# A gated mix of a recurrent memory attention and a softmax attention: output projection in column tiles, last-token batches moved, exp steps from the prologue on

## The chip, the cores and the metric

The kernel runs on one core of one Trainium2 chip. The metric is the device time of one execution in microseconds (us). Three runs of the kernel before gave 2069.38, 2077.07 and 2085.11 us, so the median is 2077.07 us. The five engines of the core are called here as the profile calls them: PE (TensorE matmuls; PEld is its weight loads), DVE (VectorE), ACT (ScalarE), POOL (GpSimd) and SP (SyncE, which here only issues transfers).

## The reference, cut to what matters

There are two attentions over the same input x of 2048 tokens by 576 features, and a gate that mixes them.

```
# A: 64 segments of 32 tokens, one after the other; mem is 8 rows of 576
for s in range(64):
    h = concat([mem, x[s*32:(s+1)*32]])            # 40 x 576
    q, k, v = h @ Wq, h @ Wk, h @ Wv               # 32 heads of 128
    p = softmax(mask(q @ k.T * 128**-0.5))         # 40 x 40 per head
    o = (p @ v) @ Wo                               # 40 x 576
    mem = o[:8]                                    # needed by the next segment
    out_a[s*32:(s+1)*32] = o[8:]
# B: 32 heads of 18 over all 2048 tokens
q, k, v = split(x @ wqkv)
out_b = concat_heads(softmax(q @ k.T * 18**-0.5) @ v) @ wo
g = sigmoid((x * gate_w).sum(-1))
out = g * out_a + (1 - g) * out_b
```

A is a recurrence: a segment can't start before the eight memory rows of the one before are there. B has no such chain.

## The kernel before, in words

**Prologue.** It loads x, transposes it on PE (`ptx`), and projects it to the q, k and v of B (lines 218 and 244). Results go to DRAM (`qtd`, `ktd`, `vgd`). The last 8 tokens of each segment don't need the memory, so their q, k and v of A are computed here for all 64 segments, in four batches of 16 segments (lines 268 and 284), and stored as `vld`, `qld`, `kld`. The weights of A (14 MB in all) are loaded on the SP queue.

**Recurrence.** Each of the 64 segments handles 32 columns (8 memory rows and the first 24 tokens) and loads the other 8 tokens. It projects six times with `project` (line 462: 20 matmuls of 512 columns in four column tiles of 32, result `pvv`, copied to `tm` on DVE), turns q and k with PE transposes (`pt`), sends v through a transfer to `v_sb` (line 492), and forms the scores (`psh`) and their exponentials on ACT. The softmax follows in two halves b: sums (`pss`), reciprocals `rq` on DVE, their spread (`prb`), a product on DVE (line 546), and the values (`pso`), copied to `ot` on DVE (line 560). The output projection then runs 160 matmuls (line 569, `pbw`): for each of 32 heads five loads of 128x128 weights `wo`, each followed by a matmul of 40 columns. Three small DVE copies (lines 582 to 584) put the memory rows into the next segment's input `ht`; line 588 keeps the other rows in `otsg`, and every fourth segment `otsg` is turned (`pto`) and stored.

**Work of B between.** `b_steps` is a generator with 1024 steps. A step has two matmuls (`sb`, line 347) and one exponential of 128x1024 on ACT (line 356, about one us); every second step has four matmuls with the values (`ob`, line 328). `tick()` is called 16 times in a segment and takes 1024/65/16 = 0.98 steps on average. Eight times in the program the next group of heads is loaded, three transfers of 512 KB each on the POOL queue. All steps are over by the end of the recurrence.

**Epilogue.** For each of 16 tiles of tokens it reloads B's output (`otn`), multiplies with `wo` of B (line 620, `po`), mixes and stores.

**Order.** Each engine runs its own list of instructions strictly in order. A scheduler sets these lists when the program is built: it takes the program's operations by their dependences and its own estimates, so that neighbours in the code may change places. PSUM has three buffers for all tiles with the tag `pb`, two for `sb`, one for `ob`.

## Time and profile before

| | us |
|---|---|
| median of three runs | 2077.07 |
| the profiled execution's own time | 2076.26 |
| its span | 2074.6 |
| start to the first segment | 283 |
| 64 segments | 1738 |
| after the last output projection | 54 |

The three stages are read from the chain of waits: the first `pvv` starts at 282.7 us and the last `pbw` ends at 2021.0 us. The page's row PEclk gives the clock that PE was granted, as a share of full speed. A view by windows gives the same share, and each engine's busy time, for any stretch of the span. The busy time of PE counts a matmul until its end, so that a full PE is not PE at its best rate; the chain of waits, which gives how long a run of matmuls held the next one up, is used for durations.

### The profile page before, as it was taken

The numbers are of one execution on the slowest core, as the hardware profiler recorded it, in microseconds if no ns is written. First come the engines' busy times: TensorE is split into PE (matmuls) and PEld (weight loads), VectorE is DVE, ScalarE is ACT, GpSimd is POOL, SyncE is SP. The second block draws the span as 40 slices with busy tenths as digits, with TensorE's granted clock in tenths as the row PEclk, the third lists the DMA queues.
The fourth block names the chain that finished last, engine by engine and source line by source line (L and its number), as shares of the span: only waits on it lengthen the run. The fifth ranks groups of instructions, "written<-read, shape, count | busy, mean of one in ns | idle before, by whom it ended". The sixth has DMA issues, their size and how long they took to land.

```text
span 2074.6 us, 67963 instructions
## 1 busy us (share of the span) xinstructions
PE 1929.8 (93%) x30629; PEld 1081.4 (52%) x30646; DVE 831.7 (40%) x1867; ACT 1119.7 (54%) x1282; POOL 107.0 (5%) x268
## 2 busy tenths in 40 slices
PE   4699979999999899999999999999999999999996
PEld 2257845555555555555555555555555555555553
DVE  5123324443444344433444344444444444333445
ACT  1122256665556556555666566656665666565660
POOL 3000010000000000000000000000000000000000
PEclk9899988888888888888888899888889988888999
DMA  8643350001000110110000100010001000100016
GB/s 256 242 133 117 123 185 26 25 26 51 24 25 26 53 29 22 29 47 20 26 25 26 56 26 26 26 56 26 24 26 55 27 23 25 52 23 23 22 42 165
DMA packets 122582, 117.31 MB, mean 57 GB/s; under 512 B 60204, under 2 KB 112116, under 8 KB 119220
## 3 DMA queue, kind: packets, MB, share of 16 engines
q1 hardware_dynamic: 97940, 90.51, 13.9%
q10 hardware_dynamic: 20896, 9.87, 2.0%
q0 software_dynamic: 3456, 12.58, 1.8%
q8 instruction: 240, 3.93, 0.8%
q14 instruction: 50, 0.41, 0.1%
HBM read 58.91 MB, written 37.22 MB: 46 GB/s over the span
## 4 chain that ended last, share of the span: by engine, by line
PE 81%; DMA 9%; ACT 4%; DVE 3%; SPq 1%; issue 1%; POOL 0%; ACTq 0%; DVEq 0%
PE pvv L462 21%; PE pbw L569 16%; PE sb L347 15%; PE ob L328 9%; ACT etb L356 4%; PE pq L284 3%; PE psh L508 3%; PE pq L218 3%; PE pt L478 3%; DMA v_sb<-tm 3%; PE pso L552 2%; PE pq L268 2%; SPq L492 1%; PE prb L538 1%; DMA otn<-otd 1%
## 5 line engine op out<-in xcount | busy, mean ns | idle before, releaser
L356 ACT ACTIVATE etb<-sb 128x1024 bf16<-128x1024 f32 x1024 | 1029.9, 1026 | 690.4 <-PE sb L347 689.2
L347 PE MATMUL sb<-qtg,ktg 32*128 32x512 bf16 x2048 | 436.8, 423 | 16.4 <-DMA ktg<-ktd 11.2
L471 DVE CAST tm<-pvv 128x512 bf16<-128x512 f32 x384 | 265.3, 691 | 286.1 <-PE pvv L462 275.4
L569 PEld LDWEIGHTS <-wo 128*128 128x128 bf16 x10240 | 328.3, 106 | 77.0 <-issue 75.0
L569 PE MATMUL pbw<-ot,wo 128*128 128x40 bf16 x10240 | 355.7, 194 | 0.0
L462 PEld LDWEIGHTS <-ht 128*32 128x32 bf16 x7680 | 187.5, 96 | 191.3 <-issue 49.6
L328 PE MATMUL ob<-etb,vgi 128*32 128x512 bf16 x2048 | 243.9, 433 | 25.7 <-ACT etb L356 21.8
L347 PEld LDWEIGHTS <-ktg 32*128 32x128 bf16 x2048 | 99.9, 92 | 222.9 <-issue 192.1
L582 DVE CAST ht<-pbw 128x32 bf16<-128x32 f32 x63 | 12.0, 191 | 388.8 <-PE pbw L569 388.8
L560 DVE CAST ot<-pso 128x320 bf16<-128x320 f32 x256 | 115.3, 485 | 97.9 <-PE pso L552 97.6
L462 PE MATMUL pvv<-wv_m,ht 128*32 128x512 bf16 x2048 | 147.4, 382 | 0.0
L462 PE MATMUL pvv<-wq_m,ht 128*32 128x512 bf16 x2048 | 138.6, 385 | 1.4 <-DVE ht L582 0.3
L328 PEld LDWEIGHTS <-vgi 128*32 128x32 bf16 x2048 | 69.8, 94 | 127.1 <-issue 111.2
L462 PE MATMUL pvv<-wk_m,ht 128*32 128x512 bf16 x2048 | 134.6, 380 | 0.0
L454 POOL COPY qt<-xl 128x256 bf16<-128x256 bf16 x64 | 26.2, 410 | 1484.1 <-PE psh L508 1403.8
L218 PE MATMUL pq<-xT,wpk 128*128 128x512 bf16 x313 | 74.9, 399 | 19.2 <-ACT stg L228 16.8
L546 DVE TENSOR_TENSOR et<-et,prb 128x320 bf16<-128x320 bf16 x128 | 62.5, 488 | 75.1 <-PE prb L538 75.1
L552 PEld LDWEIGHTS <-v_sb 64*128 64x128 bf16 x2048 | 59.7, 99 | 56.9 <-issue 45.3
L552 PE MATMUL pso<-et,v_sb 64*128 64x40 bf16 x2048 | 73.6, 187 | 15.6 <-DVE et L546 8.0
L518 DVE TENSOR_TENSOR et<-et,cap 128x320 bf16<-128x320 bf16 x128 | 42.0, 329 | 114.7 <-ACT et L516 114.6
L508 PEld LDWEIGHTS <-kt 128*64 128x64 bf16 x2048 | 64.3, 111 | 35.8 <-issue 34.7
L508 PE MATMUL psh<-qt,kt 128*64 128x40 bf16 x2048 | 80.0, 189 | 0.2 <-DVE kt L483 0.2
(103 smaller groups left out, 1472.6 us busy)
## 6 DMA issues: line engine op xcount, KB each, us to landing
v_sb<-tm SPq DMA_DIRECT2D x512, 32.0 KB
wo<-in_A_Wo_dram SPq DMA_DIRECT2D x4, 1152.0 KB
wv_m<-in_A_Wv_dram SPq DMA_DIRECT2D x4, 1024.0 KB
wq_m<-in_A_Wq_dram SPq DMA_DIRECT2D x4, 1024.0 KB
wk_m<-in_A_Wk_dram SPq DMA_DIRECT2D x4, 1024.0 KB
qtd<-stg SPq DMA_DIRECT2D x8, 512.0 KB
ktd<-stg SPq DMA_DIRECT2D x8, 512.0 KB
vgd<-vt ACTq DMA_DIRECT2D x16, 256.0 KB
```

What stands on the lines that cost most here:

```text
L218: nc.tensor.matmul(pq[:, :], lhsT=wpk[:, c, :, :].rearrange("p j e -> p (j e)"), rhs=xT[:, c, t * QC:(t + 1) * QC], start=(c == 0), stop=( ...
L284: nc.tensor.matmul(pv[:, o:o + P], lhsT=lw, rhs=xL[:, cc, q * P:(q + 1) * P], start=(c == 0), stop=(c == NF),)
L328: mm = nc.tensor.matmul(ob[32 * j:32 * j + 32, :], lhsT=vg[:, kb * P + 32 * j:kb * P + 32 * j + 32], rhs=ets[j // 2][:, j % 2, :], start=( ...
L347: nc.tensor.matmul(sb[:, i, :], lhsT=ktg[32 * j:32 * j + 32, kb * P:(kb + 1) * P], rhs=qtg[32 * j:32 * j + 32, qc * QC:(qc + 1) * QC], sta ...
L356: nc.scalar.activation(out=etb[:, :, :], in_=sb[:, :, :], func=ACT.Exp, scale=scale_b)
L462: nc.tensor.matmul(pv[32 * j:32 * j + 32, :], lhsT=ht[:, cc, :], rhs=rw, start=(c == 0), stop=(c == NF), tile_position=(0, 32 * j),)
L471: nc.vector.tensor_copy(out=tm[:, :], in_=pv[:, :])
L508: nc.tensor.matmul(psh[64 * jj:64 * jj + 64, i * L:(i + 1) * L], lhsT=kt[:, h * L:h * L + 64], rhs=qt[:, h, :], start=True, stop=True, til ...
L546: nc.vector.tensor_tensor(out=et[:, b, :], in0=et[:, b, :], in1=prb[:, 0:W8], op=ALU.mult)
L552: nc.tensor.matmul(pso[:, i * L:(i + 1) * L], lhsT=v_sb[64 * jj:64 * jj + 64, b * 1024 + i * Dh:b * 1024 + (i + 1) * Dh], rhs=et[64 * jj:6 ...
L560: nc.vector.tensor_copy(out=ot[:, j * HG:(j + 1) * HG, :].rearrange("p h t -> p (h t)"), in_=pso[:, 0:W8])
L569: nc.tensor.matmul(pbw[:, c * L:(c + 1) * L], lhsT=wo[:, h, d0:d0 + P], rhs=ot[:, h, :], start=(h == heads[0] and c == 0), stop=(h == head ...
```

## The change

**Output projection (`out_project`, `split`, `fold`).** Now the 32 columns of `ot` are the stationary operand and `wo` streams. Four heads go side by side in four column tiles, so that partition block j of the result holds a partial sum over a quarter of the heads. It is done for 384 columns of the output and then for 192, each with 32 matmuls. `split` writes the sums as a bfloat16 value and a bfloat16 remainder (two DVE operations for each of the two spans), and `fold` adds the four blocks and transposes in one go: ten matmuls of 32 columns with a constant `sel`. The last 8 rows of a segment are not projected with it. They are kept in `otl`, and `finish_group` projects those of four segments together, in the softmax of the segment after.

**Last-token batches (`last_tokens`).** Only the first batch of 16 segments is computed ahead of the recurrence. The other three are cut in 72 pieces (five matmuls of 512 columns, or 20 of 128), which `fill()` puts into the softmax: one ahead of the first half (there `finish_group` takes its place when a group is pending) and one within it. There are 64 x 2 - 15 = 113 such places; when the 72 pieces are used up, the other 41 get four matmuls into a tile `idle` that nobody reads.

**Steps of B.** They start in the prologue: 56 in `project_qk`, 8 in `project_vb`, 24 beside the first batch, 88 in all. 32 are left for the epilogue, and a segment has (1024 - 88 - 32)/64 = 14.1. Keys and values are loaded in pieces of 128 KB, partly during the block before; the end of a block (`tq` to `stage`) is done in two halves on DVE.

**Prologue.** x is loaded ahead of all else, with eight buffers instead of four; copies of the transposed x go out on POOL's queue; each load of a weight of A is put behind one of the first 18 stores on SP's queue. The gate's sum is computed by 80 one-column matmuls instead of on DVE.

**Epilogue.** Tiles of tokens are mixed while the last 32 steps of B run; B's output is loaded by blocks of 512 tokens, and the last block is used without the way through DRAM. Each tile is handled in two halves of 288 columns.

In the lists, the change moves these things on DVE. The first place is the softmax of a segment about the middle of the program. `tm` is the result of a projection, `rq` the reciprocals, `et` the weights, `ot` the attention's output. Before:

```order
L471 CAST tm_20239<-pvv_20218 128x512
L533 RECIPROCAL rq_20258<-pss_20254 128x4
L534 RECIPROCAL rq_20258<-pss_20254 64x2
L546 TENSOR_TENSOR et_2858<-et_2858,prb_20261 128x320
L560 CAST ot_2862<-pso_20274 128x320
L560 CAST ot_2862<-pso_20284 128x320
```

and in the change, where `vl` is the copy of a piece of the last-token batches:

```order
L625 CAST tm_16666<-pvv_16645 128x512
L276 CAST vl_16698<-pv_16677 128x4x16x8
L692 RECIPROCAL rq_16706<-pss_16702 128x4
L693 RECIPROCAL rq_16706<-pss_16702 64x2
L705 TENSOR_TENSOR et_2490<-et_2490,prb_16709 128x320
L276 CAST vl_16747<-pv_16726 128x4x16x8
L721 CAST ot_2494<-pso_16750 128x320
L721 CAST ot_2494<-pso_16760 128x320
```

One copy now stands ahead of the reciprocals and one ahead of the copies of `ot`. On PE the matmuls of the first piece stand ahead of `pss`, those of the second between `prb` and `pso`. The second place is the end of a segment. `ht` is the next segment's input and `otsg` keeps the segment's output rows. Before, the copies follow the projection's result `pbw` at once:

```order
L560 CAST ot_2862<-pso_20333 128x320
L582 CAST ht1_2854<-pbw_20352 128x4x8
L583 CAST ht1_2854<-pbw_20352 64x8
L584 CAST ht1_2854<-pbw_20352 64x8
L588 CAST otsg_19413<-pbw_20352 128x5x32
L471 CAST tm_20577<-pvv_20556 128x512
```

and in the change the four operations of `split` come between, on the sums `acc`, with `hl` as value and remainder:

```order
L721 CAST ot_2494<-pso_16306 128x320
L551 CAST hl_16158<-acc_16246 128x384
L552 TENSOR_TENSOR hl_16158<-acc_16246,hl_16158 128x384
L551 CAST hl_16158<-acc_16352 128x192
L552 TENSOR_TENSOR hl_16158<-acc_16352,hl_16158 128x192
L738 CAST ht0_2484<-pw3_16401 128x4x8
L739 CAST ht0_2484<-pw3_16401 64x8
L740 CAST ht0_2484<-pw3_16401 64x8
L744 CAST otsg_15871<-pw3_16401 128x5x24
L625 CAST tm_16447<-pvv_16426 128x512
```

The next segment's input now waits for two more stages, DVE's `split` and PE's `fold` (`pw3`). The diff, cut to its core:

```diff
+    sel = const.tile([P, CT], BF16, name="sel")
+    for j in range(4):
+        nc.vector.tensor_copy(out=sel[32 * j:32 * j + 32, :], in_=ident[32 * j:32 * j + 32, 32 * j:32 * j + 32])
...
+        def load_kv(g, kc):
+            kch[g, kc] = bint.tile([P, KC * P], BF16, name="kch", bufs=6)
+            nc.gpsimd.dma_start(out=kch[g, kc][:, :], in_=ktd[g, :, kc * KC * P:(kc + 1) * KC * P])
+            vch[g, kc] = bint.tile([P, KC * P], BF16, name="vch", bufs=6)
+            nc.gpsimd.dma_start(out=vch[g, kc][:, :], in_=vgd[g, :, kc * KC * P:(kc + 1) * KC * P])
+        def load_q(i):
+            if i < GB * NQC:
+                g, qc = divmod(i, NQC)
+                qch[i] = bint.tile([P, QC], BF16, name="qch", bufs=3)
+                nc.gpsimd.dma_start(out=qch[i][:, :], in_=qtd[g, :, qc * QC:(qc + 1) * QC])
...
+                    if jp == 0 and before is not None:
+                        values(kb - 1, before)
+                        if g + 1 < GB and qc == NQC - 2 and kb in (1, 2):
+                            load_kv(g + 1, kb - 1)
+                        if g + 1 < GB and qc == NQC - 1 and kb in (KC, 2 * KC):
+                            load_kv(g + 1, kb // KC + 1)
+                    yield
...
+            stage = bint.tile([P, QC], BF16, name="stage")
+            HC = QC // 2
+            for hf in range(2):
+                tq = bint.tile([P, HC // 32, 32], FP32, name="tq")
+                nc.vector.transpose(
+                    out=tq[:, :, :].rearrange("p b e -> p (b e)"), in_=ob[:, hf * HC:(hf + 1) * HC]
+                )
+                rtb = bint.tile([P, HC // 32, 1], FP32, name="rtb")
...
+            if gq == GB * NQC - 1:
+                last_stage.append(stage)
+            else:
+                nc.sync.dma_start(out=otd[:, g, qc * QC:(qc + 1) * QC], in_=stage[:, :])
...
+    def last_tokens(q, share):
+        xlb = fil.tile([P, NF + 2, P], BF16, name="xlb", bufs=1)
+        nc.sync.dma_start(out=xlb[:, :, :].rearrange("p c t -> p (c t)"), in_=xld[q])
+        for b in range(HD // 512):
+            pv = ps_a.tile([P, 512], FP32, name="pv", tag="pb")
+            for c in range(NF + 1):
+                rw, cc = w_slice(wv, c, b * 512, 512)
+                nc.tensor.matmul(pv[:, :], lhsT=xlb[:, cc, :], rhs=rw, start=(c == 0), stop=(c == NF))
+            vl = fil.tile([P, 512], BF16, name="vl")
+            copy_out(vl[:, :], pv[:, :], share)
+            nc.sync.dma_start(out=vld[q * P:(q + 1) * P, b * 512:(b + 1) * 512], in_=vl[:, :])
+            yield
+        for w, dstd in ((wq, qld), (wk, kld)):
+            for b in range(H // 4):
+                pv = ps_a.tile([P, 512], FP32, name="pv", tag="pb")
...
+                nc.sync.dma_start(
+                    out=dstd[q].rearrange("p (s f) -> p s f", s=SG)[:, :, 4 * b * LO:4 * (b + 1) * LO],
+                    in_=vl[:, :].rearrange("p (s f) -> p s f", s=SG),
+                )
+                yield
...
+        def store(out, in_):
+            d = nc.sync.dma_start(out=out, in_=in_)
+            w = next(wgen, None)
+            if w is not None:
+                issue_behind(w, d)
...
+                    store(dstd[g, :, t * QC:(t + 1) * QC], stg[:, :])
+                    if ticks != 2:
+                        b_advance(1)
...
+                if ticks != 2 and kb % 2 == 1:
+                    b_advance(1)
...
+        project_qk(0, 2)
+        project_vb(0, 2)
...
+        for g in range(1, 4):
+            project_qk(g, 4)
+        project_vb(1, 4)
+        for g in range(4, GB):
+            project_qk(g, 4)
...
+    for _ in last_tokens(0, 4):
+        b_advance(1)
...
+    def later_tokens():
+        for q in range(1, n_seg // SG):
+            yield from last_tokens(q, 0)
+    later = later_tokens()
+    def fill():
+        if next(later, "end") == "end":
+            pv = ps_a.tile([P, 512], FP32, name="idle", tag="pb")
+            for c in range(NF):
+                nc.tensor.matmul(
+                    pv[:, :], lhsT=ident[:, :], rhs=wv[0][:, c, 0:512], start=(c == 0), stop=(c == NF - 1)
+                )
...
-    b_advance(total_steps // (n_seg + 4))
...
-    per_tick = total_steps / (n_seg + 1) / 16
+    per_tick = (total_steps - done[0] - 2 * NKB) / n_seg / 16
...
+    WSPAN = ((0, 3 * P), (3 * P, Dm))
+    def out_project(acc, o, t0, b, d0, d1):
+        for i in range(4):
+            for j in range(4):
+                h = (2 * (j // 2) + b) * HG + (j % 2) * 4 + i
+                nc.tensor.matmul(
+                    acc[32 * j:32 * j + 32, 0:d1 - d0],
+                    lhsT=o[:, h, t0:t0 + CT],
+                    rhs=wo[:, h, d0:d1],
+                    start=(b == 0 and i == 0),
+                    stop=(b == 1 and i == 3),
+                    tile_position=(0, 32 * j),
+                    skip_group_check=True,
+                )
+    def split(acc, hl, d0, d1):
+        nc.vector.tensor_copy(out=hl[:, 0, d0:d1], in_=acc[:, 0:d1 - d0])
+        nc.vector.tensor_tensor(
+            out=hl[:, 1, d0:d1], in0=acc[:, 0:d1 - d0], in1=hl[:, 0, d0:d1], op=ALU.subtract
+        )
+    def fold(hl):
+        pw3 = ps_a.tile([P, NF + 1, CT], FP32, name="pw3", tag="pb")
+        for c in range(NF + 1):
+            d0 = c * P if c < NF else T0
+            for part in range(2):
+                nc.tensor.matmul(
+                    pw3[:, c, :], lhsT=hl[:, part, d0:d0 + P], rhs=sel[:, :], start=(part == 0), stop=(part == 1)
+                )
+        return pw3
...
+    def finish_group():
+        if not pending:
+            return
+        s, otsg = pending.pop()
+        hll = seg2.tile([P, 2, Dm], BF16, name="hl")
+        for d0, d1 in WSPAN:
+            accl = ps_a.tile([P, 512], FP32, name="acc", tag="pb")
+            for b in range(2):
+                out_project(accl, otl, 0, b, d0, d1)
+            split(accl, hll, d0, d1)
+        pwl = fold(hll)
...
+        if pending:
+            finish_group()
+        else:
+            fill()
...
+            if b == 0:
+                fill()
...
-        heads = [j * HG + i for j in (0, 2, 1, 3) for i in range(HG)]
-        pbw = ps_a.tile([P, 512], FP32, name="pbw", tag="pb")
-        for h in heads:
-            for c in range(NF + 1):
-                d0 = c * P if c < NF else T0
-                nc.tensor.matmul(
-                    pbw[:, c * L:(c + 1) * L],
-                    lhsT=wo[:, h, d0:d0 + P],
-                    rhs=ot[:, h, :],
-                    start=(h == heads[0] and c == 0),
-                    stop=(h == heads[-1] and c == NF),
-                    skip_group_check=True,
-                )
-            if heads.index(h) % 8 == 7:
-                tick()
-        pw3 = pbw[:, 0:(NF + 1) * L].rearrange("p (c t) -> p c t", t=L)
+            if b == 0:
+                acc0 = ps_a.tile([P, 512], FP32, name="acc", tag="pb")
+            out_project(acc0, ot, 0, b, *WSPAN[0])
+            tick()
+        split(acc0, hl, *WSPAN[0])
+        acc1 = ps_a.tile([P, 512], FP32, name="acc", tag="pb")
+        for b in range(2):
+            out_project(acc1, ot, 0, b, *WSPAN[1])
+            tick()
+        split(acc1, hl, *WSPAN[1])
+        pw3 = fold(hl)
...
+        nc.vector.tensor_copy(out=otsg[:, :, i4 * seg:i4 * seg + CT - M], in_=pw3[:, :, M:CT])
+        nc.gpsimd.tensor_copy(out=otl[:, :, i4 * LO:(i4 + 1) * LO], in_=ot[:, :, CT:L])
...
+        if qc == NQC - 1:
+            b_advance(1 << 30)
+            o_last = last_stage[0]
+        else:
+            while done[0] < ((GB - 1) * NQC + qc + 1) * NKB * 2 + 1:
+                b_advance(1)
+            nc.sync.dma_start(
+                out=ofs[qc][:, GB - 1:GB, :], in_=otd[:, GB - 1:GB, qc * QC:(qc + 1) * QC]
+            )
...
+            for d0 in (0, Dm // 2):
+                d1 = d0 + Dm // 2
+                po = ps_a.tile([P, 512], FP32, name="po", tag="pb")
+                for g in range(GB):
+                    lw = o_last if g == GB - 1 and qc == NQC - 1 else ofs[qc][:, g, :]
+                    nc.tensor.matmul(
+                        po[:, 0:Dm // 2],
+                        lhsT=lw[:, i:i + P],
+                        rhs=wop[:, g, d0:d1],
+                        start=(g == 0),
+                        stop=(g == GB - 1),
+                    )
...
+            if qc < NQC - 1:
+                b_advance(2)
...
```

410 lines of the change are left out of this document (197 added, 213 removed).

## The prediction

> **What bounds the kernel now.** I read the page first, then windows by stage, then the chain of waits.
>
> ```profile
> PE 1929.8 (93%) x30629; PEld 1081.4 (52%) x30646; DVE 831.7 (40%) x1867; ACT 1119.7 (54%) x1282; POOL 107.0 (5%) x268
> PEclk9899988888888888888888899888889988888999
> 0.00:283.00 283.00, 220.98 (x2024) 146.07 (x2035) 87.77 (x157) 65.99 (x134) 28.58 (x59) 0.93 0.54 179
> 283.00:2021.00 1738.00, 1672.07 (x28347) 918.24 (x28346) 714.59 (x1672) 1052.65 (x1148) 78.47 (x209) 0.86 0.11 33
> 2021.00:2074.00 53.00, 36.74 (x261) 17.12 (x266) 29.34 (x38) 1.02 (x1) 0.00 (x0) 0.94 0.61 162
> ```
>
> In a window row stand the stretch, its length, the busy time of PE, PEld, DVE, ACT and POOL, then PE's clock, the DMA share and GB/s. PE is the bound, and 1738 of 2074.6 us are the 64 segments, where its clock is 0.86. Next, segment by segment (62 windows from one write of `ht` to the next; the first, the last and the sum):
>
> ```profile
> 318.49:344.08 25.59, 25.29 (x444) 13.77 (x442) 11.86 (x28) 16.51 (x18) 1.05 (x3) 0.93 0.12 34
> ...
> 1966.43:1991.11 24.68, 23.78 (x444) 13.40 (x442) 12.05 (x29) 16.50 (x18) 0.75 (x2) 1.00 0.07 21
> sum 1672.62, PE 1610.45 PEld 887.35 DVE 693.49 ACT 1009.77 POOL 77.42; mean PE 25.97 PEld 14.31 DVE 11.19 ACT 16.29 POOL 1.25
> ```
>
> The mean segment takes 1672.62/62 = 26.98 us, the one at clock 1.00 takes 24.68. Where the clock goes is seen in stretches of 3.41 us, the length at which it changes:
>
> ```profile
> 958.61:962.03 3.42, 3.32 (x47) 1.55 (x43) 1.85 (x6) 2.69 (x5) 1.06 (x3) 1.00 0.15 40
> 962.03:965.44 3.41, 3.21 (x51) 1.70 (x47) 1.73 (x7) 2.78 (x4) 0.00 (x0) 0.98 0.27 75
> 965.44:968.85 3.41, 3.31 (x66) 2.35 (x67) 0.89 (x2) 1.55 (x2) 0.00 (x0) 0.50 0.09 24
> 968.85:972.27 3.42, 3.42 (x78) 2.49 (x74) 0.00 (x0) 1.13 (x2) 0.00 (x0) 0.52 0.00 0
> 972.27:975.68 3.41, 3.35 (x74) 1.88 (x76) 1.10 (x5) 2.05 (x2) 0.00 (x0) 1.00 0.02 5
> ```
>
> The stretch from 962.03 is the softmax, with its short matmuls and waits; the next two, over the output projection, run at half clock. That it repeats is what the stage's 0.86 says. The chain shows what each stage costs at full clock (first fence) and at half (second, with one long wait):
>
> ```profile
> 1978.29 1.19 PE pvv L462 x20
> ...
> 1981.18 0.50 DVE et L546
> 1981.68 0.04 issue
> 1981.72 0.48 PE pso L552 x16
> ...
> 1983.15 1.03 ACT etb L356
> ...
> 1985.36 1.10 PE pbw L569 x40
> 1986.47 0.32 PE sb L347 x2
> ...
> 1988.21 0.33 PE ob L328 x4
> ...
> 1994.96 1.08 PE pvv L462 x20
> ...
> 1998.21 1.00 PE pt L478 x16
> ```
>
> ```profile
> 907.91 1.45 PE pbw L569 x40
> 909.36 0.54 PE sb L347 x2
> ...
> 929.59 7.11 DMA v_sb<-tm
> ```
>
> Columns are start, length, what. A quarter of the projection takes 1.45 us instead of 1.10, a `sb` pair 0.54 instead of 0.32.
>
> The Trainium skill ("TensorE: Matmul & The Clock Gate", Part 1) says that the clock is either half or full, decided in windows of about 3.4 us, and that an idle window halves it. The trace agrees on the two values and the length, but not on the cause: ahead of the fall PE was busy 3.21 of 3.41 us. By the page's rule no window of the changed segment would be idle, all would run at full clock, and the sum below would end at 1884 us instead of 1897.
>
> **The change, segment by segment.** The base is the segment of 24.68 us. Its waits are 0.50 (DVE), 1.03 (ACT) and about 0.1 of issue, 1.63 in all, so PE's work is 23.05.
>
> Removed: the projection, 4 x 1.10 = 4.40. Moved out: 16 - 14.1 = 1.9 steps of B at 0.32 + 0.33/2 = 0.485, so 0.92. Left: 17.73.
>
> `out_project`: per segment 64 matmuls in 16 groups of four column tiles. `pvv` is the same shape, five groups of 512 columns in 1.08 us, 0.216 each. By columns, eight groups of 384 take 1.30 us and eight of 192 take 0.65, so 1.95 at least. Short matmuls don't go below 0.48/16 = 0.030 us each with their load (`pso`), so a group of 192 takes 0.12, and the sum is 1.30 + 0.96 = 2.3, which I take. The upper bound is 64 x 1.08/20 = 3.5, if a load and a matmul always need what they need in `pvv`.
>
> `fold`: ten pairs, between 1.10/40 = 0.0275 (`pbw`) and 1.00/16 = 0.0625 (`pt`) each, 0.28 to 0.63; I take 0.5. Fills: the rows of the prologue, below, give 5 x 8.36/38 = 1.10 and 20 x 17.87/320 = 1.12 for a piece, and 4 x 0.22 = 0.88 for an idle one; 0.1 more for the change of shape (1.19 against 1.08 at `pvv`). That is (72 x 1.2 + 41 x 1.0)/64 = 2.0. `finish_group`: 2.3 + 0.5 and 1.2 of waits for its own `split`, 16 times: 1.0 a segment. PE's work: 17.73 + 2.3 + 0.5 + 2.0 + 1.0 = 23.5 us, no less than before.
>
> Waits. DVE's prices:
>
> ```profile
> L471 DVE CAST tm<-pvv 128x512 bf16<-128x512 f32 x384 | 265.3, 691 | 286.1 <-PE pvv L462 275.4
> L582 DVE CAST ht<-pbw 128x32 bf16<-128x32 f32 x63 | 12.0, 191 | 388.8 <-PE pbw L569 388.8
> L546 DVE TENSOR_TENSOR et<-et,prb 128x320 bf16<-128x320 bf16 x128 | 62.5, 488 | 75.1 <-PE prb L538 75.1
> L588 DVE CAST otsg<-pbw 128x160 bf16<-128x160 f32 x64 | 20.8, 325 | 6.1 <-PE pbw L569 4.4
> ```
>
> Between 325 ns for 160 columns and 691 for 512, 192 columns take 0.36 us, and the subtraction about as much (488 for 320 is on the same line). After the last `acc` PE thus waits 0.72 for both; the `sb` and `ob` that stand there (0.32 and 0.33) and the parts of `fold` that are ready leave 0.3. The three `ht` copies (none over 0.19, so about 0.5) wait behind one `sb` pair: 0.2. The 0.50 on `et` is covered by the fill of 1.2 that now stands there. The wait for ACT stays, with fewer steps: 0.8. The sum is 1.3, and the segment 24.8.
>
> Clock. A half-clock stretch costs at most 3.41/2 = 1.7 us. Each softmax half now holds about 1.1 us of unbroken full matmuls. I take this to lift most stretches over the bar and leave one fall in ten segments, 0.2. So 25.0, and 64 x 25.0 = 1600 us. The long waits such as 7.11, when a group's 1.5 MB is loaded, go too: the loads are twelve times smaller, and the fills stand in front of the second `pso`. If the cover fails, that costs what the mean segment shows, next part but one.
>
> **Prologue and epilogue.**
>
> ```profile
> 0.00:80.00 80.00, 34.24 (x158) 16.54 (x161) 28.68 (x61) 13.14 (x40) 18.41 (x40) 0.84 0.89 286
> 93.18 10.74 PE pq L218 x49
> 156.44 2.61 PE L244 MATMUL pq<-wb,xT 128*128 128x288 bf16 x20 [0.73 <-DVE vt L254]
> 153.13 2.68 DMA vgd<-vt
> 163.52 8.36 PE pq L268 x38
> 171.88 17.87 PE pq L284 x320
> 270.58 8.18 DMA ktg<-ktd
> ```
>
> The first 80 us are bound by transfers: 286 GB/s at a share of 0.89. x, the weights, the transposed x, and B's first q, k and v with their way back are about 25.7 MB by the sizes of the tiles, 90 us at that rate. SP's queue is in order, so a store of `vgd` waits behind a weight of 1 MB, and its buffer with it; if this adds up (16 x 2.68/2 = 21 us after the last weight), it is 105; if the order only does as well as before, 80. PE's work in it is hidden. What follows is PE's: 280 `pq` at 10.74/49 = 61 us, 80 `pvb` at 2.61/20 = 10.4, one batch 8.6 + 17.9 = 26.5, 67 steps of B at 0.485 = 32.5, and 60 changes of shape at 0.1 = 6: 136. Then the wait for the first segment's loads, 8.18 before; 6 now. Together 232 us (218 to 260), where 283 stood. Of the four batches (4 x 26.4 us) three have moved into the segments, where the fills count them.
>
> ```profile
> 2038.09 3.08 DMA otn<-otd
> 2041.22 2.15 PE po L620 x16
> ```
>
> Before, each tile of the epilogue waits about 3 us and then works 2.15. Now: the last `finish_group` 4, eight steps bound by ACT while the first blocks load 9, 256 matmuls of 288 columns at 0.131 = 33.5, 24 steps at 0.485 = 11.5, and a tail of DVE (four operations each half), mixing and store of about 5: 63 us (54 to 75), where 53.6 stood. The 32 steps in it left the segments.
>
> Total: 232 + 1600 + 63 + 1.7 around the span = 1897 us. It stands against 2076.26, the profiled run, which is 0.8 below the median of 2077.07; I leave that out.
>
> **Rivals.**
>
> Everything covered. All waits but 0.5 vanish, the clock stays full: 24.0 a segment, and the low ends outside: 218 + 1536 + 56 + 2 = 1812. For it: PE's work is 23.5; against: the wait for ACT, which fills don't cover. Chance 0.17.
>
> The clock still falls. The stretches are free-running, and the softmax keeps its short matmuls; the stretch that set off the fall was 94% busy by the profile, so I don't know the bar. Then the difference of mean and full-clock segment, 26.98 - 24.68 = 2.3, stays: 27.1 a segment, 232 + 1734 + 63 + 2 = 2031. Chance 0.17.
>
> Weight loads bind `out_project`. At 3.5 instead of 2.3 in 80 projections: 1897 + 96 = 1993. Against it: `pso` manages 0.030 with loads of 128 columns. Chance 0.08. The Trainium skill ("TensorEngine Tiling (Array Packing)", Gotcha 2) speaks for it: column tiling excludes the fast weight load. No run here shows the load of a column tile by itself.
>
> Slower: the idle place moves to the segment's end. `split`, `fold` and `ht` are one serial chain on the recurrence. If `sb` and `ob` don't stand in its gaps, its wait is 1.6 instead of 0.5, and the half clock then falls on the projections, which are full matmuls and pay it whole: two stretches, 3.4. 24.8 + 1.1 + 3.4 = 29.3, in all 232 + 1875 + 63 + 2 = 2172. It is slower than before from (2076 - 297)/64 = 27.8 us a segment on. Against it: the lists have a `sb` pair on both sides of `fold`. Chance 0.07.
>
> **How the numbers follow.** The forecast has 0.51, with its own range of 1850 to 1950; it and the first three rivals are all faster. A measurement of this kernel can tell about 1% from no change, here 2056 to 2098. The case of the falling clock reaches into this with its upper end (0.04). So faster 0.89, same 0.04, slower 0.07. The range goes from 1805, with half of the first rival left out, to 2030, with the upper half of the second and the slower case left out: 0.08 below and 0.16 to 0.2 above.
>
> **What would show it.** PEclk near 1.0 in the segments, and no 0.50 after the softmax; segments of about 25.0; `acc` 2.3 us a segment in the chain, `fold` 0.5; first `pvv` at 232; 63 us after the last segment; no `v_sb` wait over 2 us. I am wrong in the main step if the clock stays at 0.86, in the cost of PE if segments at full clock take over 26, and in the cover if the chain shows DVE's `hl` with more than 1 us a segment.

## The result, and the profile after

The changed kernel takes 2010.09 us (median of 4 runs, 2002.94 to 2010.77), the kernel before, beside it, 2076.55 us. The ratio is 0.967 with a 95% interval of 0.963 to 0.971: 3.3% faster, 66 us, where 180 were forecast. The time lies inside the range, the forecast of 1897 us was 113 us too low. The profiled run took 2010.2 us, its span 2008.5.

The page of the changed kernel (its first line and the granted clock), then windows by stage: up to the first projection of the first segment, the 64 segments, the epilogue. Columns are as in the prediction.

```profile
PE 1880.2 (94%) x26570; PEld 963.3 (48%) x26570; DVE 1019.9 (51%) x2416; ACT 1083.6 (54%) x1222; POOL 175.1 (9%) x409
PEclk9599999999988999999999999989998999999979
0.00:260.00 260.00, 206.43 (x1376) 96.26 (x1380) 74.75 (x154) 112.98 (x157) 39.49 (x77) 0.87 0.60 177
260.00:1925.00 1665.00, 1614.86 (x24789) 834.76 (x24784) 904.82 (x2176) 939.91 (x1033) 135.60 (x332) 0.98 0.16 37
1925.00:2008.00 83.00, 58.90 (x421) 32.29 (x413) 40.28 (x87) 30.71 (x32) 0.00 (x0) 0.79 0.42 118
```

PE's share of busy time has hardly moved (93 to 94%). What moved is the clock at which it is busy: 0.98 over the segments, where 0.86 stood. The three stages miss the forecast all on the same side: 260 us against 232 (+28), 1665 against 1600 (+65), 83.5 up to the span's end against 63 (+20).

Segment by segment (62 windows from one write of `ht` to the next; three that end a group of four, three plain ones between them, and the sum):

```profile
1297.77:1330.52 32.75, 32.55 (x456) 17.54 (x452) 14.94 (x35) 15.59 (x18) 1.45 (x4) 0.79 0.11 24
1330.52:1355.20 24.68, 24.06 (x363) 11.77 (x355) 14.40 (x36) 13.59 (x16) 2.03 (x5) 1.00 0.14 39
1355.20:1380.06 24.86, 24.39 (x364) 11.96 (x360) 11.95 (x28) 14.55 (x17) 1.45 (x4) 1.00 0.08 20
...
1405.40:1433.49 28.09, 27.80 (x439) 14.18 (x435) 14.29 (x35) 14.77 (x17) 1.45 (x4) 1.00 0.09 23
...
1643.23:1667.15 23.92, 23.04 (x360) 11.20 (x363) 12.09 (x29) 13.96 (x16) 1.54 (x4) 1.00 0.11 29
...
1820.66:1849.18 28.52, 28.23 (x440) 14.11 (x436) 14.29 (x34) 15.36 (x17) 1.45 (x4) 1.00 0.08 23
sum 1612.43, PE 1563.68 PEld 809.40 DVE 877.81 ACT 907.98 POOL 132.32; mean PE 25.22 PEld 13.05 DVE 14.16 ACT 14.64 POOL 2.13
```

The mean is 1612.43/62 = 26.0 us. Of the 47 plain segments 43 run at clock 1.00, in 23.1 to 26.4 us, 24.66 on average. The 15 in which `finish_group` stands are the long ones: 27.7 to 28.8 us at full clock, 28.24 on average, and 29 to 33 where the clock falls, which happens in six of 15. The longest of all is a plain one (600.00:634.05, 34.05 us, clock 0.80): there PE waits 4.1 us in the chain for `xlb`, the input of a batch, and the clock falls. What happens at the end of a group shows in the timeline of PE (one row), the chain of waits, and stretches of 3.41 us, all of the first segment of that table:

```profile
1309.43 2.14 PE L540 MATMUL acc<-wo,otl 128*32 128x384 bf16 x64
```

```profile
1310.96 0.57 DVE hl L551
...
1311.55 0.57 DVE hl L552
...
1312.17 0.29 PE pw L561 x5
...
1313.75 0.34 DVE otsg L580
...
1314.14 0.58 PE pto L587 x5
```

```profile
1306.74:1310.15 3.41, 3.41 (x64) 1.61 (x66) 1.34 (x3) 2.98 (x5) 1.05 (x3) 1.00 0.21 55
1310.15:1313.57 3.42, 3.33 (x69) 1.82 (x61) 1.74 (x4) 1.11 (x2) 0.00 (x0) 1.00 0.22 56
1313.57:1316.98 3.41, 3.31 (x29) 1.84 (x29) 1.34 (x5) 2.37 (x3) 0.00 (x0) 0.61 0.16 53
1316.98:1320.39 3.41, 3.41 (x40) 2.29 (x38) 1.55 (x4) 0.00 (x0) 0.00 (x0) 0.50 0.00 0
```

The projection of the group's last tokens is dense and takes 2.14 us. Behind it stands a serial chain: copy, subtract, ten small products, copy, five transposes, and the first sums of the next softmax. The clock falls right behind it and stays at one half for about four stretches.

In the prologue and the epilogue the trace shows transfers. The first rows are windows of the prologue. Then come SP's queue (start, length, what is issued), the same issues one by one (ns: least, median, most), and DVE's copies into the buffers of these stores (count, busy time, ns of one, then its idle time and what ended it). The last three are the chain of waits in the epilogue:

```profile
40.00:105.00 65.00, 37.64 (x168) 14.26 (x167) 5.00 (x13) 22.78 (x31) 4.81 (x9) 0.56 0.78 266
105.00:228.00 123.00, 116.30 (x660) 46.36 (x659) 48.04 (x91) 63.37 (x74) 5.53 (x8) 0.97 0.44 136
228.00:262.00 34.00, 27.58 (x361) 20.85 (x364) 8.61 (x15) 16.79 (x20) 0.95 (x3) 0.91 0.59 71
```

```profile
231.22 13.42 SPq L306 DMA_DIRECT2D qld<-vl x7
```

```profile
L306 SPq DMA_DIRECT2D qld<-vl x8: 512/513/599, 228.9 to 244.1; - x8
```

```profile
L276 DVE CAST vl<-pv 128x512 bf16<-128x512 f32 x18 | 12.3, 686 | 37.5 <-DMA qld<-vl 12.5 <-DMA vld<-vl 10.1 <-DMA kld<-vl 6.8
```

```profile
1936.63 6.93 DMA wop<-in_B_wo_dram
1943.59 8.36 DMA wop<-in_B_wo_dram
1952.00 13.89 PE po L783 x96
```

Up to 105 us PE works 65 us out of 105, and its clock falls to 0.56. From 231 on a store of last-token results goes out every 13.42/7 = 1.9 us, in rows of 64 bytes (four heads of eight tokens). SP's own issue is 0.51 us of that; the rest is waiting. DVE's copies wait for one of the two buffers, that is for earlier stores to land, 29 us in all. The short rows show in the transfers: 71 GB/s at a share of 0.59 from 228 us on, where 266 GB/s took 0.78 before. In the epilogue the first `po` starts 27 us after the last segment, 15.3 of them waiting for B's output weights.

### The profile page after: what moved, and what is told of

It reads as the page before. It is cut to its first block, busy times and chain, and to the rows that moved or that the text cites. A ratio compares the mean times of both kernels' runs of the same rounds, so it can differ in the third digit from the quotient of the medians.

```text
span 2008.5 us, 60909 instructions
## 1 busy us (share of the span) xinstructions
PE 1880.2 (94%) x26570; PEld 963.3 (48%) x26570; DVE 1019.9 (51%) x2416; ACT 1083.6 (54%) x1222; POOL 175.1 (9%) x409
## 3 DMA queue, kind: packets, MB, share of 16 engines
q8 instruction: 208, 3.41, 0.7%
## 4 chain that ended last, share of the span: by engine, by line
PE 74%; DVE 6%; issue 3%; ACT 2%; DMA 1%; ACTq 0%; SPq 0%; DVEq 0%; POOL 0%
PE pvv L616 22%; PE sb L210 14%; PE acc L540 9%; PE ob L190 7%; PE psh L662 3%; PE pt L632 3%; PE pv L297 3%; PE prb L697 3%; PE pw L561 2%; ACT etb L219 2%; PE idle L470 2%; PE pso L713 2%; DVE ot L721 2%; PE po L783 2%; PE pv L285 2%
## 5 line engine op out<-in xcount | busy, mean ns | idle before, releaser
L210 PE MATMUL sb<-qch,kch 32*128 32x512 bf16 x2048 | 442.5, 395 | 18.6 <-ACT etb L219 12.6
L616 PEld LDWEIGHTS <-ht 128*32 128x32 bf16 x7680 | 197.2, 97 | 202.9 <-issue 45.8
L190 PE MATMUL ob<-etb,vch 128*32 128x512 bf16 x2048 | 235.8, 399 | 24.8 <-ACT etb L219 16.0
L540 PE MATMUL acc<-wo,ot 128*32 128x384 bf16 (+1 forms) x4096 | 204.6, 299 | 9.7 <-DVE ot L721 3.2
L210 PEld LDWEIGHTS <-kch 32*128 32x128 bf16 x2048 | 105.0, 91 | 218.5 <-issue 195.1
L540 PEld LDWEIGHTS <-ot 128*32 128x32 bf16 x4096 | 116.5, 99 | 85.3 <-DVE ot L721 48.2
L190 PEld LDWEIGHTS <-vch 128*32 128x32 bf16 x2048 | 68.4, 94 | 112.5 <-issue 88.6
L276 DVE CAST vl<-pv 128x512 bf16<-128x512 f32 x90 | 62.0, 690 | 106.2 <-PE pv L297 39.7
L551 DVE CAST hl<-acc 128x384 bf16<-128x384 f32 (+1 forms) x160 | 72.4, 452 | 77.3 <-PE acc L540 76.6
L552 DVE TENSOR_TENSOR hl<-acc,hl 128x384 bf16<-128x384 f32 (+1 forms) x160 | 72.9, 456 | 5.1
```

Source lines behind the costliest of these rows:

```text
L190: mm = nc.tensor.matmul(ob[32 * j:32 * j + 32, :], lhsT=vc[:, o + 32 * j:o + 32 * j + 32], rhs=ets[j // 2][:, j % 2, :], start=(kb == 0), ...
L210: nc.tensor.matmul(sb[:, i, :], lhsT=kc[32 * j:32 * j + 32, o:o + P], rhs=qch[gq][32 * j:32 * j + 32, :], start=True, stop=True, tile_posi ...
L540: nc.tensor.matmul(acc[32 * j:32 * j + 32, 0:d1 - d0], lhsT=o[:, h, t0:t0 + CT], rhs=wo[:, h, d0:d1], start=(b == 0 and i == 0), stop=(b = ...
L551: nc.vector.tensor_copy(out=hl[:, 0, d0:d1], in_=acc[:, 0:d1 - d0])
L552: nc.vector.tensor_tensor(out=hl[:, 1, d0:d1], in0=acc[:, 0:d1 - d0], in1=hl[:, 0, d0:d1], op=ALU.subtract)
L616: nc.tensor.matmul(pv[32 * j:32 * j + 32, :], lhsT=ht[:, cc, :], rhs=rw, start=(c == 0), stop=(c == NF), tile_position=(0, 32 * j),)
```

## The experiments

Times are medians, ratios are to the kernel before, each with its 95% interval; the changed kernel stands at 2010.09 us and 0.967. Differences to it that are below 10 us are not told apart from none, and 11 us is at the edge.

**What holds the clock: three runs.** First, the batches in the prologue again and nothing in the softmax places:

```
     later = later_tokens()
+    for q in range(1, n_seg // SG):
+        for _ in last_tokens(q, 2): pass
     def fill():
-        if next(later, "end") == "end": (idle products)
+        return
```

> The changed kernel with all four last-token batches in the prologue and nothing in the two softmax places of a segment. Theory (the fills hold the clock; the projection itself buys little): the segments fall back to a granted clock near 0.87 and 26 to 27 us, and the prologue is 60 to 80 us longer, so about 2090, the time of the kernel before. Rival (the gain came from the four-column-tile projection): the clock falls but the run stays below 2030, since only the 41 idle fills are gone and the batches merely move.

Measured: 2178.73 us, ratio 1.052 (1.046 to 1.058): slower than the kernel before by 5%. Neither number was right. The windows of that run (the added batches, then its segments):

```profile
262.00:408.00 146.00, 120.25 (x1222) 77.81 (x1220) 27.01 (x43) 52.50 (x68) 4.15 (x8) 0.91 0.49 74
408.00:2090.00 1682.00, 1624.62 (x23356) 804.18 (x23356) 861.52 (x2098) 904.34 (x998) 131.64 (x324) 0.88 0.11 30
```

The three batches take 146 us in the prologue, of which the chain has 68 in waits for their stores (46.7 for `qld`, 21.7 for `kld`), so the 5% overstate what the fills are worth. The segments show it cleanly: relieved of 72 pieces of batches and 41 idle ones, they take 1682 us, 17 us more than the changed kernel's 1665. At 0.88 instead of 0.98, PE loses more than 113 fills cost. So the three batches cost nothing in the segments.

Then the changed kernel with the batches in their places, but no idle products:

```
-        if next(later, "end") == "end": (idle products)
+        next(later, None)
```

> The changed kernel without its 41 idle fills (the dummy products that stand where no last-token batch is left; late in the recurrence those places are empty again). Theory (dense work in the two softmax places is what keeps the clock up): the segments from about number 25 on fall back to a granted clock of 0.85 to 0.9 and grow from 24.9 to 26 or more, so the run is 10 to 50 us slower than the changed kernel although 41 us of PE work are gone. Rival (the idle products are only a cost): the clock stays near 1.0 and the run is about 40 us faster, near 1970.

Measured: 2021.04 us, ratio 0.973 (0.969 to 0.976); 11 us slower although 164 products are gone, at the edge of what can be told and inside the theory's 10 to 50. Windows of two late plain segments, at full clock and not, and of all its segments:

```profile
1551.90:1573.66 21.76, 21.12 (x350) 10.81 (x342) 11.94 (x29) 13.55 (x16) 1.45 (x4) 1.00 0.12 32
...
1596.31:1622.68 26.37, 25.73 (x356) 12.70 (x352) 11.94 (x28) 14.43 (x17) 1.45 (x4) 0.81 0.07 20
```

```profile
258.00:1939.00 1681.00, 1626.28 (x24596) 840.06 (x24588) 903.29 (x2175) 939.11 (x1033) 135.58 (x332) 0.94 0.16 37
```

The pieces last to about segment 41, not to 25 as expected, and up to 40 the plain segments but one are as in the changed kernel. Of the 17 plain segments behind that, six are at full clock and take 21.1 to 23.9 us; the others have a clock of 0.76 to 0.87 and take 25.5 to 28.0. What decides between the two was not found. With two idle fills the same 17 take 23.9 to 25.7. The means are 25.2 and 24.8, so the price of the idle fills and what they gain by the clock nearly cancel.

Last, idle products alone in the kernel before, two per segment at the same two places:

```
+        idle()          # 4 products of 512 columns, ahead of the sums
         for b in range(2):
             ...
+            if b == 0: idle()   # ahead of the products with v
```

> The kernel before, with two idle fills in each segment at the two softmax places (four products of 512 columns each, 0.9 us at full clock; their results go nowhere) and nothing else. Theory (the falls of the clock come from the thin work there): the granted clock of the segments goes from 0.86 to 0.95 or more and a segment stays at 26 to 27 us although it holds 1.9 us more of PE work, so 2010 to 2080. Rival (the clock falls for another reason, such as the 40-column products of the projection): the clock stays at 0.86 to 0.88 and the run is 100 to 140 us slower, 2180 to 2220.

Measured: 2080.70 us, ratio 1.001 (0.998 to 1.004). A window over its segments, and the group of the idle products (count, busy time, ns of one):

```profile
276.00:2020.00 1744.00, 1702.71 (x28777) 914.15 (x28778) 719.14 (x1673) 1061.90 (x1151) 80.75 (x214) 0.95 0.12 35
```

```profile
L439 PE MATMUL idle<-wv_m,ident 128*128 128x512 bf16 x512 | 133.6, 382 | 0.0
```

134 us of PE work were added, and the time is the same: the clock rose from 0.86 to 0.95 and paid for all of it. The rival, the short products of the old projection, is out as the main cause of the falls: they are all still in this kernel.

**What the projection is worth: two runs.** The changed kernel with the old projection, and nothing left over for the group's end, so that a fill stands in these 15 places too:

```
-            out_project(acc0, ot, 0, b, *WSPAN[0]) ... split ... fold
+        for h in heads:                        # 32 heads
+            for c in range(NF + 1):            # 5 pieces of the row
+                nc.tensor.matmul(pbw[:, c * L:(c + 1) * L], lhsT=wo[:, h, d0:d0 + P], rhs=ot[:, h, :], ...)
```

> The changed kernel with the output projection of the kernel before put back (160 products that write the projection transposed, 40 columns each, no four tiles, no split, no fold, and no projection left to a group's end: the end of a group only transposes and stores). The fills, the idle products and the exp work from the prologue on stay. Theory (at a full clock the new projection buys next to nothing): 1990 to 2030, within 1% of the changed kernel. Rival (it saves what the prediction's sum says, 4.40 less 2.3, 0.5, 0.3 and 1.0 in a segment, and the old form lets the clock fall on top): 2030 to 2120.

Measured: 2021.00 us, ratio 0.974 (0.970 to 0.978). So 55 of the 66 us come with the old projection too, and the new one adds 11, at the edge of what can be told. The groups of both kernels over their segments (count, busy time), the changed one first:

```profile
L540 PE MATMUL acc<-wo,ot 128*32 128x384 bf16 (+1 forms) x4096 | 204.6, 299 | 9.7 <-DVE ot L721 3.2
L561 PE MATMUL pw<-sel,hl 128*128 128x32 bf16 x790 | 65.7, 181 | 3.9 <-DVE hl L551 0.5 <-DVE hl L552 0.2
L540 PE MATMUL acc<-wo,otl 128*32 128x384 bf16 (+1 forms) x1018 | 34.4, 287 | 0.0
```

```profile
L716 PE MATMUL pbw<-ot,wo 128*128 128x40 bf16 x10240 | 314.7, 186 | 0.2 <-issue 0.2
```

204.6 + 65.7 + 34.4 = 304.7 us against 314.7. That the difference of 10 us is near that of the times proves little: the run with the old projection has 15 idle fills more, and no `split` to wait for.

To price it by itself, half of its products were left out:

```
     def out_project(acc, o, t0, b, d0, d1):
-        for i in range(4):
+        for i in (0, 3):
```

> The changed kernel with half the products of the output projection left out (heads 1, 2, 5, 6 of each eight add nothing), in the segments and at a group's end: 32 of the 64 products of 80 projections, everything else as it was. It prices the projection. By the prediction's 2.3 us for a projection: 80 x 1.15 = 92 us faster, about 1918. By the 248 us that the profile of the changed kernel has PE busy on it (3.1 each): 80 x 1.55 = 124 us, about 1886. Rival (other work runs beside it, B's steps above all, so that it is in part hidden): under 70 us, over 1940.

Measured: 1942.75 us, ratio 0.935 (0.930 to 0.940), 67 us for half of 80 projections. That is the rival's number, but not for its reason. In three segments at full clock (the first windows, whose counterparts took 23.92, 23.95 and 25.09) the half is worth (72.96 - 69.43)/3 = 1.18 us, and over all 37 plain segments that are at full clock in both runs 0.96 on average; the 2.3 for a whole one says 1.15. The rest goes in new falls (fourth window): the clock is below full in 17 of the 62 segments, where the changed kernel has 10.

```profile
1579.62:1601.75 22.13, 21.22 (x320) 10.31 (x322) 12.01 (x29) 11.93 (x14) 1.54 (x4) 1.00 0.12 33
1601.75:1625.32 23.57, 22.88 (x335) 10.88 (x331) 11.76 (x28) 14.93 (x17) 1.99 (x5) 1.00 0.10 26
1625.32:1649.05 23.73, 23.18 (x335) 10.85 (x331) 14.29 (x36) 15.02 (x18) 2.52 (x7) 1.00 0.13 38
...
1698.88:1725.64 26.76, 26.55 (x328) 11.39 (x324) 11.94 (x29) 14.78 (x17) 1.45 (x4) 0.82 0.08 19
```

**What the end of a group costs: two runs.** Its projection left out:

```
-        for d0, d1 in WSPAN: (out_project, split)
-        pwl = fold(hll)
-        nc.vector.tensor_copy(out=otsg[...], in_=pwl[...])
+        nc.vector.tensor_copy(out=otsg[...], in_=otl[...])
```

> The changed kernel without the projection of the last tokens at a group's end: its products, split and fold are left out, and the end of a group copies other numbers into their rows, transposes and stores. It prices that part where it stands. By the prediction's 2.3 + 0.5 + 1.2 for each of the 16: 64 us faster, 1946. Theory (it costs more than its work, since it is a serial chain and the clock falls behind it in five of 15 places): 80 us or more faster, 1930 or less. Rival (its PE work alone, 2.8 each): 45 us, about 1965; and where nothing dense stands in its place the clock may fall in those segments, which would make it less.

Measured: 1930.39 us, ratio 0.928 (0.924 to 0.932): 80 us, 5.0 for each of the 16, the theory's number. Its PE work alone would be 45. The sum of its 62 segments, where the changed kernel has 1612.43:

```profile
sum 1533.48, PE 1482.92 PEld 765.61 DVE 850.04 ACT 907.01 POOL 132.79; mean PE 23.92 PEld 12.35 DVE 13.71 ACT 14.63 POOL 2.14
```

Then the same work in other places:

```
+    def place(s, k):                  # k: the first or second softmax place
+        if s >= 4 and s % 4 == 0: finish_a(k); return      # column span k: products and split
+        if s >= 4 and s % 4 == 1: finish_fold() if k == 0 else finish_out()
+        fill()
```

> The changed kernel with the end of a group cut into four pieces that stand in the softmax places of two segments: its two column spans in segment 4k (one in each place, instead of a fill), its fold and its transposes and store in segment 4k+1 (ahead of the fill there). The same work, but 15 idle fills fewer, and no piece waits for its own split. Theory (the end of a group costs 4.6 us more than a plain segment because it is one serial chain that also lets the clock fall in a third of its places): 50 to 70 us faster, 1940 to 1960, and no segment at a clock near 0.8. Rival (it is PE work that has to be done anyway): only the 15 idle fills go, 10 to 20 us, 1990 to 2000.

Measured: 1944.83 us, ratio 0.936 (0.932 to 0.939): 65 us faster than the changed kernel with the same output and the same products, but 15 idle fills fewer. Windows: a segment that holds two of the pieces, and all segments:

```profile
1659.18:1684.03 24.85, 24.85 (x420) 12.73 (x416) 13.46 (x32) 14.77 (x17) 2.51 (x6) 1.00 0.12 31
```

```profile
259.20:1859.00 1599.80, 1557.40 (x24696) 807.05 (x24692) 902.16 (x2175) 941.85 (x1033) 135.38 (x332) 1.00 0.16 39
```

One short fall is left (963.06:989.12, clock 0.94), and a segment with a piece of a group's end in each place is no longer than a plain one (24.8 us on average, a plain one 24.9): there the products are fill. The 15 segments with a group's end take 69 us less in all; the ones behind them, which now hold the fold and the transposes, take 1.0 us more each. The rival (PE work that must be done anyway, 10 to 20 us) is out. Free the four pieces are not: the run stands 14 us above the one that leaves the group's end out, 0.9 each, and has 15 idle fills fewer than that one.

**The wait for `ot`.** The chain of the changed kernel gives DVE's copies of `ot` 2.2% of the 1665 us, 0.57 a segment: the projection stands right behind the products whose copies it needs. In this run both softmax halves come first, then the fill, then all products with v, then the projection:

```
-        for b in range(2): sums, reciprocals, scaling; fill if b == 0; products with v; out_project(acc0, ot, 0, b, ...)
+        for b in range(2): sums
+        for b in range(2): reciprocals
+        for b in range(2): scaling
+        fill()
+        for b in range(2): products with v
+        for b in range(2): out_project(acc0, ot, 0, b, ...)
```

> The changed kernel with the softmax and what follows it in another order: both halves' sums and reciprocals first, then the fill, then all four products with v, and only then the output projection of both halves. The same instructions. PE waits for DVE's ot 0.57 us a segment in the changed kernel (its first projection stands right behind the products whose copies it needs), which the prediction's sum left out. Theory: that wait goes, a plain segment at full clock falls from 24.9 to 24.3 or less, 35 to 60 us faster. Rival (the time comes back as a wait for v, which is needed 3 us earlier, or as a fall of the clock over the softmax that now has only one fill in its middle): within 10 us, or slower.

Measured: 1998.37 us, ratio 0.961 (0.957 to 0.965), 12 us faster, near the rival's size. Two windows of it, a plain segment and the end of a group:

```profile
1350.37:1374.11 23.74, 23.20 (x363) 11.44 (x360) 11.77 (x28) 14.67 (x17) 1.46 (x4) 1.00 0.08 21
...
1496.36:1526.78 30.42, 29.40 (x438) 15.10 (x435) 16.41 (x43) 14.56 (x17) 3.20 (x7) 0.83 0.14 40
```

The counterpart of the first took 24.86 us, but that is one of the larger gains: over the 43 plain segments at full clock in both runs it is 0.27 us on average. The chain over the segments says where the rest went. Its part for `ot` fell from 37.2 to 3.4 us, so the wait itself is gone; its part for ACT's exp rose from 32.5 to 69.1, and 26 us now stand for v (`v_sb` and its issue), 2 before. The clock falls in eight of the 15 ends of groups. So the theory had the wait right and not its worth, and the rival had both of its mechanisms, but not the largest, ACT.

**Prologue and epilogue: three runs.** The last weights on SP's queue, ahead of B's result (`nc.scalar.dma_start` to `nc.sync.dma_start` for `wop`):

> The changed kernel with the last weights (wop) issued on SP's queue, ahead of the three blocks of B's result (of), instead of on ACT's. Theory (the 15.3 us of waiting for wop in the epilogue come from the two loads sharing the transfer engines, with the weights in the small pieces): the wait shrinks to 5 us or less, 10 to 15 us faster. Rival (the data as a whole arrive no sooner, and the wait moves to of): within 5 us of the changed kernel.

Measured: 1992.20 us, ratio 0.959 (0.955 to 0.963), 18 us faster. Its chain has no wait for `wop` any more, as the theory says. But only about 8 us lie in the epilogue, which takes 1988.1 - 1912.6 = 75.5 us in its trace, and there ACT's exp is now the largest entry behind PE (19.3% of the chain from 1905 us on). The rest stands elsewhere: the first segment starts 3 us earlier, and two segments fewer have a fall of the clock.

Five buffers instead of two for the last-token results (`bufs=5` for `vl`):

> The changed kernel with five buffers instead of two for the last-token results on their way out (vl). Theory (in the prologue's last batch DVE and ACT wait 29 us for stores of 1.9 us each, in pieces of 64 bytes, and PE waits for them at 228 to 260): PE no longer waits for a buffer, 5 to 12 us faster. Rival (SP's queue issues one such store in 1.9 us and is the limit in any case): within 3 us of the changed kernel.

Measured: 1996.85 us, ratio 0.960 (0.956 to 0.964), 13 us faster. The first projection of the first segment, in the timeline of the changed kernel and in the chain of this one:

```profile
259.67 1.90 PE L616 MATMUL pvv<-wq_m,ht 128*32 128x512 bf16 x16 [1.12 <-DVE ht L506]
```

```profile
249.41 2.34 PE pvv L616 x40
```

10 us of the gain stand there. The rival is out: SP's issue (0.51 us) was not the limit, the two buffers were. The recurrence's weights on ACT's queue (`nc.scalar.dma_start` in `load_weights`, no order behind the stores):

> The changed kernel with the weights of the recurrence (three loads of 1 MB each and two small ones, for each of three matrices) issued on ACT's queue instead of SP's, so that no store of B's q, k and v stands behind a megabyte in the same queue. Theory (PE's clock of 0.5 to 0.6 and its waits between 40 and 105 us come from the stores that stand behind the weights): the first segment starts 15 to 20 us earlier, 1990 to 1995. Rival (the transfers as a whole bind that stretch, whatever the queue): within 5 us of the changed kernel.

Measured: 2005.60 us, ratio 0.965 (0.961 to 0.968), not told apart from the changed kernel. Windows of the two kernels, this one second:

```profile
0.00:105.00 105.00, 64.55 (x377) 29.98 (x377) 18.11 (x49) 33.77 (x66) 33.01 (x66) 0.73 0.78 258
```

```profile
0.00:105.00 105.00, 62.02 (x364) 31.83 (x369) 22.74 (x56) 23.46 (x56) 35.88 (x71) 0.82 0.81 270
```

The rate is about the same (258 and 270 GB/s), and PE has done no more work by 105 us. The order in the queues was not the cause. That the transfers as a whole are was not shown: it fits up to 80 us, where the changed kernel's DMA share is 0.88 and this run's 0.89, but from 80 to 105 it is only 0.48 and 0.52, and what holds PE there stays open.

**Together: four runs.** The cut group's end, `wop` on SP's queue and six buffers for the prologue's batch, in a pool of their own:

> Three of the corrections together: the end of a group cut into pieces in the softmax places, the last weights on SP's queue ahead of B's result, and six buffers for the last-token results of the prologue's batch. Theory (the three losses are separate, in segments, epilogue and prologue): their gains add up, 65 + 18 + 13 = 96 us, so about 1914. Rival (they cover each other, the prologue's for one, since the first segment waits for something else too): 1925 to 1940.

Measured: 1933.06 us, ratio 0.930 (0.928 to 0.933). The chain at the start of the first segment:

```profile
248.64 4.67 DMA kld<-vl
...
260.51 10.51 DMA xl<-kld
```

The first segment began at 248 us, but stood 10.5 us for a load behind `wo`, which the pool had pushed back. So `wo` came first in the next run:

```
+    wo = aw2.tile(...); its four loads
     with tc.tile_pool(name="fil0", bufs=6, side="right") as fil0:
         for _ in last_tokens(0, 4, fil0): b_advance(1)
-    wo = aw2.tile(...); its four loads
```

> The three corrections together once more, with the recurrence's output weights (wo, 4.6 MB) loaded before the last-token batch of the prologue, as the changed kernel has them; in the first form they came behind it, and the first segment stood 10.5 us behind them. Theory (the three losses are separate and that wait is all that was lost): the first segment takes 28 to 30 us instead of 41.8, and the run 1915 to 1922. Rival (the batch's stores then wait behind wo, and the wait returns ahead of the first segment): 1930 or more.

Measured: 1930.57 us, ratio 0.927 (0.924 to 0.930). The wait went, and another came, ahead of the first segment, which began at 257:

```profile
210.93 10.34 DMA vld<-vl
```

So the rival holds: `wo` and the batch's stores want the same stretch, and in either order one waits some 10 us. More buffers gain nothing beside the other two; 1944.83 - 18 would be 1927. Both forms once more with the other order of softmax and projection:

> The three corrections and the other order of the softmax and the projection. Theory (the wait for ot stands alone): 35 to 60 us faster than the three together, 1855 to 1880. Rival (with the end of the group in the softmax places, the one before the products with v no longer lies between the two halves, and the clock falls there): no faster than the three.

> The same with the other order of the softmax and the projection. Theory: 15 to 20 us faster than the three together, as in the first form (1933.06 and 1914.48), so about 1897 to 1903. Rival: over 1910.

Measured: 1914.48 us, ratio 0.922 (0.919 to 0.924), and 1917.14 us, ratio 0.921 (0.917 to 0.926): 19 and 13 us less than the three, where 35 to 60 were expected of the first, 15 to 20 of the second. The first lines of the chain, of the second form without and with the other order, say where the rest went:

```profile
PE 85%; DVE 6%; DMA 4%; ACT 2%; issue 2%; SPq 0%; ACTq 0%; DVEq 0%; POOL 0%; POOLq 0%
```

```profile
PE 84%; ACT 6%; DMA 5%; DVE 3%; issue 1%; SPq 0%; ACTq 0%; DVEq 0%; POOL 0%; POOLq 0%
```

DVE's 3% went, and 4% of ACT came. In the chain over the segments the part for `ot` falls from 34.0 to 3.9 us, and that for ACT's exp (1.03 us each) rises from 16.3 to 93.3: PE now waits for the exponentials of B's steps. The four in the first form are the fastest version run, 164 us below the kernel before beside it (2078.66).

## Why the prediction was right and wrong

The main mechanism, the projection and the fills came as forecast. What failed is the rest of the sum, in all three stages on the same side: the segment at 25.0 (65 us too little), the prologue at 232 (28) and the epilogue at 63 (20). In the segment, the sum has 17.73 + 2.3 + 0.5 + 1.3 and two fills of 1.13 for a plain one, 24.1 us, and 27.0 where a group's end of 4.0 replaces one fill. At full clock 24.66 and 28.24 were measured, 0.57 and 1.28 more. The falls of the clock cost 0.48 a segment (26.01 for the mean of all, 25.53 if all were as those at full clock) and not 0.2. Over 64 segments that is 27, 20 and 18 us, together the 65. None of the forecast's three signs of being wrong came up (the clock is 0.98, segments at full clock would take 25.53 us on average and not over 26, `hl` has 0.48 us a segment in the chain): they did not watch the terms that failed.

**The clock: right in kind, too small in its length.** The forecast said that the fills would hold the clock with about one fall in ten segments, 0.2 us a segment. 0.98 was measured, 1.00 once the group's ends were spread, and 0.88 without the fills. That 134 us of idle work cost the kernel before nothing shows the mechanism by itself. The trace of the changed kernel has nine falls in the segments, but four of them last four or five stretches of 3.41 us. In all it is 75 us at half clock. The Trainium skill ("TensorE: Matmul & The Clock Gate", Part 1) says that an idle window halves the clock. The trace still disagrees on the cause: in the stretch ahead of the fall shown above the profile has PE busy 3.33 of 3.42 us. How much thin work it takes was not found.

**`out_project` at 2.3 us: right.** 2.14 us where 64 stand unbroken, 188.6/80 = 2.36 in the chain over the segments, and 0.96 to 1.18 for a half. The third rival (3.5 each) would have made the half 1.75 and is out. The Trainium skill ("TensorEngine Tiling (Array Packing)", Gotcha 2) says that column tiling excludes the fast weight load; whatever the loads do, they don't bind here. (The sum's floor of 0.030 a matmul is above the 0.0275 of its own row of `pbw`; that is 0.1 us of the 2.3.) The saving against the old form was small in the sum (4.40 removed; 2.3, 0.5 and 1.0 and their waits added), and it measures 11 us.

**Fills at 2.0 us: right.** An idle one takes 0.97 us in the chain, a piece of a batch 88.1/72 = 1.22. Five segments at full clock differ by 2.43, 2.81, 1.98, 1.96 and 1.65 us with and without their two, 2.2 on average.

**`finish_group` at 1.0 a segment: too small.** It was "2.3 + 0.5 and 1.2 of waits", 4.0 each; left out it gives back 80/16 = 5.0, its falls included. The step lacks the clock: the serial chain that the fourth rival put at the end of every segment exists in every fourth, and there it brings half clock in six of 15 cases. In the segments' own ends it does not, as forecast: only three of the nine falls begin in plain segments.

**The waits at 1.3 a segment: too small by the waits that were not in the sum.** It had `split`, `ht`, `et` and ACT. In the chain these have 0.48 (with the groups' ends), 0.07, 0.11 and 0.51 us a segment, 1.2 together, so what was counted was right. The waits for `v_sb`, 0.95 a segment before, are gone, as forecast. What was put at nothing is DVE's copies of `ot` between the products with v and the projection, 0.57, and DVE's copies `vl` of the pieces, 0.20, which the list of DVE's instructions ahead of the prediction shows in front of the reciprocals and of `ot`. Six segments without any fill, at full clock in the run without idle products, take 21.76, 22.65, 21.11, 22.36, 22.90 and 23.90 us, 22.45 on average; the sum for them is 17.73 + 2.3 + 0.5 + 1.3 = 21.8. The 0.6 between fits the 0.57 of `ot`, but the six differ by 2.8 us among themselves. That PE waits there is shown, 37 us in the chain; that these 37 us were to be had is not, since the runs with the other order gave back 12 to 19, with ACT waiting in its place. The old order had the projection behind all products; I took the neighbours of the old trace for those of the new.

**The prologue at 232: the bound was in the text, and I took the other end.** 90 us of transfers were taken, 105 named as the upper value; 105 came. But the cause named for it (stores behind a megabyte of weights) was tried and is not it; what else holds PE from 80 us on stays open. 136 of PE's work and 6 of waiting became 155: 10 of the 13 are waits for the batch's stores, now cut in eight and in rows of 64 bytes, with two buffers. They went with five buffers. The sum had no term for these stores.

**The epilogue at 63: wrong by the load.** "Eight steps bound by ACT while the first blocks load 9" became 27 us from the last segment to the first `po`, since the weights on one queue and B's result on another arrive late. Moving the weights ended that wait and gave back 8 of the 20. In the chain of that run ACT's exp stands in its place; the other 12 us were not taken apart.

**The first rival (everything covered)** needed 24.0 us a segment; no version run came under 24.6. (Its total has 56 for the epilogue, where the low end was 54.) **The second (the clock still falls)** gave 2031 and came near the time for another reason: its 27.1 us a segment were not seen. The fall itself is there in the run without fills, at 0.88 and 26.3 us a segment.

## What to carry to other kernels

On a stage that PE bounds and in which its clock falls, price thin work by the granted clock of its segment: a microsecond of dense products put into it can be free, and a microsecond of work removed can be paid back. Work that must be done somewhere is the best filler, if it is cut so that none of its pieces waits for another: the same group's end cost 5.0 us as one chain and 0.9 in four pieces that also stand in for idle fills. When code is moved, list for each instruction what it waits for in its new place, and ask who waits next when that wait is taken away: here it was ACT. And for a store that is cut, count how long it keeps its buffer and how many buffers there are, not only its bytes.
